# Keys and queries transposed on VectorE from a second load, and the last w2 slices loaded into w2's own room

## The chip, the cores and the metric

The kernel runs on one core of one Trainium2 chip. The metric is the device time of one execution in microseconds (us). Engines are named as in the profile: PE (TensorE, matmuls), PEld (its weight loads), DVE (VectorE), ACT (ScalarE), POOL (GpSimd) and SP (SyncE, which here only issues DMAs).

## The reference

A delta-rule recurrence over 4 batches, 8 heads, 768 steps and head width 48, whose output is laid out as x of 4 x 768 x 384, goes through a mixer: a low-rank mix over the sequence (U, V of rank 32) and a two-layer ReLU network of width 1536.

```python
def _attn_ref(q, k, v, beta):
    k_n = k / (np.linalg.norm(k, axis=-1, keepdims=True) + 1e-06)
    for t in range(S):
        y[:, :, t] = einsum('bhd,bhde->bhe', q[:, :, t], state)
        v_old = einsum('bhde,bhd->bhe', state, k_n[:, :, t])
        state = state + bt * einsum('bhd,bhe->bhde', k_n[:, :, t], v[:, :, t] - v_old)

def _moe_ref(x, U, V, w_ch1, w_ch2):
    h = x.transpose(0, 2, 1) @ U @ V
    u = x + h.transpose(0, 2, 1)
    return u + np.maximum(u @ w_ch1, 0.0) @ w_ch2
```

All matrices are float32 on the chip. The weights arrive as float64 and are put together from their two halves on the chip.

## The kernel before

**Units.** The recurrence is cut into chunks of L = 64 steps. A unit is half a batch, that is 6 chunks of 8 heads; units 0 to 7 are numbered n, and batch b has units 2b and 2b + 1. Keys of a unit come in by tokens (tile kn, 64 tokens by 48 numbers for each chunk and head, two heads stacked on the 128 partitions), queries likewise (qn), values too (vn).

**Within a unit.** `grams` makes the transposed keys and queries and their products. For each of three pairs of chunks, `key_pair` turns four 128x128 blocks of keys on PE against the identity (`turn`, L529, into PSUM tile p_t), ACT copies them to SBUF (L535, tile kq), and `products` multiplies keys by keys (L553, p_g), which ACT or DVE copies to pg. `query_pair` does the same with queries; DVE masks that product into qk (L569). `norms` squares the keys (L461), sums them on DVE (L464) and gets the scales, which go through DRAM (L499, L505, tiles scrc and cp) to where they are wanted. `blocks` takes pg through DRAM (L624, L635) into 96 rows of 32x32 blocks (gs), inverts these on DVE in 31 steps of two instructions (L668 prod, L674 xt; "inversion n" below), writes them to DRAM (L683), reads them back in two layouts (L707 zt, L710 zc), turns zc on DVE (L695 zn), and joins the 32-blocks into 64-blocks with two rounds of small matmuls (L722 p_x, L736 p_v), which ACT writes into zt (L746). For units 0 and 1 the inversion goes in 16-blocks, with `join` instead.

**Recurrence.** `recur(b)` walks through 12 chunks: keys and queries times state (L870, p_y), DVE takes it from the values (L900, rhs), p_s (L907), ACT copies z (L916), p_s and p_y (L921, L929), DVE adds the state (L944). It is a chain from chunk to chunk.

**Mixer.** `front(b, i)` mixes over the sequence: p_tt (L971), DVE copy tt (L977), p_tt again (L980), tt (L985), p_h (L995), DVE adds to x (L1001), PE turns x (L1005, p_u), ACT copies ut (L1008). `wide(b, i)` does the two layers on 384 tokens: 36 matmuls p_f (L1038) with ReLU on ACT, 36 p_o (L1058) with an addition on DVE (L1028) and a store by SP (L1029). The profile counts each of these float32 matmuls as two. These matmuls stand between the steps of the next batch's recurrence.

**Weights.** `load_weights` brings the weights in 14 slices (U, V, six of w1, six of w2; all but U have 768 columns) through POOL's queue, in turn into a tile of their own ("wide") and into the room of a later x ("stage", tag x). Each slice takes five DVE instructions and one on ACT. Until w2 is needed its room (`early`) holds other things: queries of unit 1, keys of unit 2, squares and small blocks. `recur(b)` for b > 0 waits for the last w2 slice, because its x takes stage's room.

**Order.** There is no scheduling at run time. A planner in the kernel (`run`) holds a clock for each engine. Every `step` states its cost, and among parts whose `need` is met the planner emits the one that can start first, with ties going to the lower place number given in `order`. So costs and places fix the order of each engine's queue once, when the kernel is built; at run time each engine takes its queue in order. SP's queue holds nearly all DMAs of keys, queries, values, of DRAM passes and of the output.

Of the kernel before, what the change touches and what calls it, by code (L numbers as in the profile page):

```python
# [27 lines left out]
def kernel(  # L28
# [157 lines left out]
    beta_sb = unit.tile([B * H, S], FP32, name="beta_sb", tag="kq")  # L186
# [94 lines left out]

    def load_weights():
# [6 lines left out]

        def start(i):  # L290
            dst, src, groups = slices[i]
            n = dst.shape[1]
            if i % 2:
                wide = stage[:, 0 : 2 * n].bitcast(I32).rearrange("p (n two) -> p n two", two=2)
            else:
                wide = conv.tile([128, n, 2], I32, name="wide")
            src = src.bitcast(I32)
            to = wide.rearrange("p n two -> p (n two)")
            if groups:
                to = to.rearrange("p (c r) -> p c r", c=groups)  # L300
                src = src.rearrange("(c p) r -> p c r", c=groups)
            copies = 128 // src.shape[0]
            yield step(pool=0.55 * copies)
            for c in range(copies):
                at = slice(c * 128 // copies, (c + 1) * 128 // copies)
                nc.gpsimd.dma_start(out=to[at], in_=src)
            loaded[i] = wide
            emitted(("landed", i), 6.0)

        def load_all():  # L310
            for i in range(len(slices)):
                yield need(("weights", i - 2), *[("v", 0)] * (i == 1), *[("opened", 1)] * (i == 2))
                yield from start(i)

        begin(load_all(), 2.03)
        for i in range(len(slices)):
            dst = slices[i][0]
            yield need(("landed", i))

            if dst.shape[1] == WIDE and i >= 2 + KT * DFF // WIDE:  # L320
                yield need(("ksq", 2), *[("keys turned", 2, c) for c in range(UC // 2)])
# [38 lines left out]
            emitted(("weights", i), 0.2)  # L360

# [54 lines left out]
    def load(n):  # L416

        yield need(("rec", n - 2))
        kq = unit.tile([128, UC, 2, 2, 2 * L], FP32, name="kq")
# [19 lines left out]
    def load_queries(n):  # L439
        yield need(("turned", n - 1), ("turned", 0))  # L440
        yield from fetch(n, "q", qn[:, :, :, 0:D], q, (0, 0))

    def norms(n):
# [8 lines left out]
        if n > 2:  # L452

            ksq = made[n][0][:, UC // 2 :].rearrange("p c j i t -> p (c j i t)")
        else:
            ksq = early[:, (1536, 2816, 0)[n] :]
# [59 lines left out]
    def grams(n, place):  # L516


        yield need(("k", n), ("room", n), ("pg", 0 if n == 1 else -1))
        kn = keys[n]  # L520
        kq, pg, qk = made[n]

        def turn(ts, places):
# [11 lines left out]
            nc.scalar.copy(places, p_t)  # L535

        def products(c0, i):
# [9 lines left out]
            for c in range(2):  # L547
                for j in range(2):
                    for par, x in QUADS:
# [5 lines left out]
                            kq[rows, c0 + c, j, 0, cols],  # L555
                            kq[rows, c0 + c, j, i, cols],
# [19 lines left out]
        def key_pair(c0):  # L576
            if n > 2 and c0 + 2 > UC // 2:
                yield need(("ksq", n))
            yield from turn([(kn, c0), (kn, c0 + 1)], kq[:, c0 : c0 + 2, :, 0])
            emitted(("keys turned", n, c0 // 2))  # L580
            yield from products(c0, 0)
            emitted(("p", n, c0 // 2), 0.5)

        def query_pair(c0):
            yield need(("q", n), ("p", n, c0 // 2))
            yield from turn([(qt, c0), (qt, c0 + 1)], kq[:, c0 : c0 + 2, :, 1])
# [13 lines left out]
        emitted(("turned", n))  # L600

# [264 lines left out]
    def recur(b):  # L866
        def from_state(p, kq, cu, i, s_old, first):

            for j, par, x in heads:
                nc.tensor.matmul(  # L870
                    p[half(x ^ par), par, D * (2 * i + j) : D * (2 * i + j) + D],
                    kq[half(par, D), cu, j, i, half(x)],
# [7 lines left out]
        yield need(("mixed", b - 2), ("rec", 2 * b - 1), w2_there(FT - 1 if b > 0 else -99))  # L880
# [198 lines left out]
    for n in range(2, 2 * B):  # L1079
        at = 0.01 * n + (3 if n < 4 else 5)  # L1080
        order += [(load_keys(n), at + 0.1), (load(n), at + 0.1), (load_queries(n), at + 0.5)]
# [39 lines left out]
```

## Time and profile before

| | |
|---|---|
| median of 8 runs | 680.02 us |
| lowest, highest | 676.44, 681.64 us |
| profiled execution | 676.58 us, of which 674.8 are the span that the profile shows |
| mean granted clock of PE | 0.919 of full speed |
| busy in the span | PE 92%, DVE 47%, ACT 29%, POOL 6% |
| chain of waits | PE 80%, DMA 7%, DVE 7% |
| DMA packets | 143893, of which 133952 on SP's queue |

The page has busy times by engine, forty equal slices of the span with a digit for the busy tenths, the chain of work that ended last, and groups of instructions by line. The trace answers more closely: instructions in order of time, with what ended an idle time in brackets, and busy times in chosen stretches. The profile is one execution, and a short one among the eight.

### The profile page before, as it was taken

How to read it: one execution, taken by the hardware profiler on the slowest of the kernel's cores; microseconds unless marked ns; L12 is line 12 of the kernel's file. 1: busy time of each engine (PE TensorE's matmuls, PEld its weight loads, DVE VectorE, ACT ScalarE, POOL GpSimd, SP SyncE). 2: the span in 40 equal slices, each digit the busy share in tenths (PEclk: the TensorE clock that was granted, in tenths of full speed). 3: DMA queues.
4: the chain of work that ended last, by engine and by line, in shares of the span. 5: the costliest groups of instructions: out<-in, count | busy, mean ns of one | idle time of the engine just before them, and what ended most of it. 6: DMA issues, size and time to landing. Idle time of an engine off the chain costs nothing.

```text
span 674.8 us, 19682 instructions
## 1 busy us (share of the span) xinstructions
PE 621.9 (92%) x8676; PEld 399.7 (59%) x8676; DVE 318.3 (47%) x795; ACT 199.0 (29%) x487; POOL 43.3 (6%) x84
## 2 busy tenths in 40 slices
PE   5639799859999999989999999999999999999997
PEld 4438688536555666556556655665655555555554
DVE  6667678579898124872942287368111011000000
ACT  2406456524221352144214322323221220110210
POOL 6442001100100000000000000000000000000000
PEclk9855555859999999999999999999999999999999
DMA  8586737742711332256033312420300000000000
GB/s 123 113 184 162 148 113 174 185 89 40 197 37 37 73 62 61 48 106 113 10 72 76 73 35 55 67 61 2 60 14 26 1 1 24 12 1 23 13 11 24
DMA packets 143893, 46.00 MB, mean 68 GB/s; under 512 B 136961, under 2 KB 140033, under 8 KB 143809
## 3 DMA queue, kind: packets, MB, share of 16 engines
q1 hardware_dynamic: 133952, 30.99, 22.6%
q0 software_dynamic: 3552, 12.88, 6.8%
q10 hardware_dynamic: 6304, 0.89, 0.8%
q8 instruction: 68, 1.11, 0.7%
q14 instruction: 17, 0.13, 0.1%
HBM read 33.62 MB, written 11.11 MB: 66 GB/s over the span
## 4 chain that ended last, share of the span: by engine, by line
PE 80%; DMA 7%; DVE 7%; ACT 2%; SPq 2%; issue 1%; ACTq 1%; DVEq 0%
PE p_o L1058 28%; PE p_f L1038 27%; PE p_y L870 4%; PE p_g L553 3%; PE p_t L529 3%; PE p_s L921 2%; PE p_s L907 2%; DMA scr<-xt 2%; PE p_y L929 2%; DVE xt L674 2%; DVE prod L668 2%; PE p_u L1005 1%; PE p_e L794 1%; DMA scr<-pg 1%; PE p_h L995 1%
## 5 line engine op out<-in xcount | busy, mean ns | idle before, releaser
L1038 PE MATMUL p_f<-ut,w_sb 128*128 128x384 f32 x576 | 202.3, 496 | 0.2 <-ACT h_f L1023 0.2
L1058 PE MATMUL p_o<-w_sb,h_f 128*128 128x384 f32 x576 | 201.1, 495 | 0.0
L1038 PEld LDWEIGHTS p_f<-ut,w_sb 128*128 128x128 f32 x576 | 104.3, 190 | 64.0 <-issue 0.6
L1058 PEld LDWEIGHTS p_o<-w_sb,h_f 128*128 128x128 f32 x576 | 104.6, 190 | 63.4
L1023 ACT ACTIVATE h_f<-p_f 128x384 f32<-128x384 f32 x96 | 47.1, 491 | 202.8 <-PE p_f L1038 202.7
L1028 DVE TENSOR_TENSOR x<-x,p_o 128x384 f32<-128x384 f32 x24 | 13.2, 553 | 131.4 <-PE p_o L1058 131.4
L674 DVE TENSOR_TENSOR xt<-xt,prod 96x112 f32<-96x112 f32 (+21 forms) x216 | 70.5, 326 | 7.4
L668 DVE TENSOR_TENSOR prod<-gs,xt 96x112 f32<-96x112 f32 (+21 forms) x216 | 70.0, 324 | 6.2
L553 PE MATMUL p_g<-kq 48*64 48x64 f32 x1536 | 40.2, 252 | 9.4 <-DVE qk L569 7.9
L944 DVE TENSOR_TENSOR s<-s,p_s 128x192 f32<-128x192 f32 x40 | 14.1, 352 | 69.2 <-PE p_s L921 68.9
L553 PEld LDWEIGHTS p_g<-kq 48*64 48x64 f32 x1536 | 33.8, 161 | 18.3 <-DVE qk L569 7.4
L951 ACT COPY x<-p_y 64x192 f32<-64x192 f32 x96 | 30.0, 313 | 39.2 <-PE p_y L929 34.0
L870 PEld LDWEIGHTS p_y<-s,kq 48*64 48x64 f32 x1408 | 28.8, 151 | 19.6 <-issue 10.9
L535 ACT COPY kq<-p_t 128x512 f32<-128x512 f32 x48 | 27.4, 587 | 38.6 <-PE p_t L529 38.4
L916 ACT COPY z<-p_s 128x192 f32<-128x192 f32 x48 | 15.3, 318 | 73.6 <-PE p_s L907 73.3
L900 DVE TENSOR_TENSOR rhs<-vn,p_y 128x192 f32<-128x192 f32 x44 | 15.5, 352 | 42.1 <-PE p_y L870 41.6
L870 PE MATMUL p_y<-s,kq 48*64 48x48 f32 x1408 | 34.3, 239 | 0.7 <-DVE s L944 0.5
L907 PEld LDWEIGHTS p_s<-rhs,zt 64*64 64x64 f32 x704 | 16.3, 148 | 21.8 <-issue 17.7
L921 PEld LDWEIGHTS p_s<-z,kn 64*64 64x64 f32 x704 | 16.0, 149 | 19.4 <-issue 16.5
L907 PE MATMUL p_s<-rhs,zt 64*64 64x48 f32 x704 | 21.9, 242 | 3.2 <-DVE qk L569 1.7
L794 PE MATMUL p_e<-zt,pg 64*64 64x32 f32 x192 | 12.0, 291 | 12.9 <-DMA zt<-scr 11.6
L637 POOL MEMSET xt<- 96x1056 f32 x6 | 5.9, 978 | 275.6 <-DMA scr<-xt 194.8
(122 smaller groups left out, 529.7 us busy)
## 6 DMA issues: line engine op xcount, KB each, us to landing
wide<-in_moe_w_ch_dram POOLq DMA_DIRECT2D x6, 768.0 KB, 5.3
stage<-in_moe_w_ch_dram POOLq DMA_DIRECT2D x6, 768.0 KB, 5.6
out_dram<-x SPq DMA_DIRECT2D x24, 192.0 KB, 2.2
kn<-in_k_dram SPq DMA_DIRECT2D x60, 72.0 KB, 2.4
qn<-in_q_dram SPq DMA_DIRECT2D x48, 72.0 KB, 3.1
vn<-in_v_dram SPq DMA_DIRECT2D x48, 72.0 KB, 2.7
gs<-scr SPq DMA_DIRECT2D x8, 384.0 KB, 4.7
scr<-xt SPq DMA_DIRECT2D x8, 384.0 KB, 4.5
```

The lines of the kernel that those rows point to most:

```text
L529: nc.tensor.transpose(p_t[:, x, j], t[:, c, 2 * j : 2 * j + 2].rearrange("p s d -> p (s d)"), ident,)
L535: nc.scalar.copy(places, p_t)
L553: nc.tensor.matmul(p_g[par][to, c, j], kq[rows, c0 + c, j, 0, cols], kq[rows, c0 + c, j, i, cols], start=True, stop=True,)
L668: nc.vector.tensor_tensor(out=prod, in0=gb[:, :, j : j + 1, j + 1 :].to_broadcast([NP, split, m, w]), in1=xb[:, :, 0:m, j : j + 1].to_broa ...
L674: nc.vector.tensor_tensor(out=xb[:, :, 0:m, j + 1 :], in0=xb[:, :, 0:m, j + 1 :], in1=prod, op=ALU.subtract,)
L870: nc.tensor.matmul(p[half(x ^ par), par, D * (2 * i + j) : D * (2 * i + j) + D], kq[half(par, D), cu, j, i, half(x)], s_old[half(par, D), ...
L907: nc.tensor.matmul(p_s[half(x), par, D * (2 + j) : D * (2 + j) + D], zt[half(x ^ par), cu, par, j], rhs[half(x ^ par), 2 * j + par], start ...
L921: nc.tensor.matmul(p_s[half(par), x, D * j : D * j + D], kn[half(x), cu, 2 * j + par], z[half(x), 2 * j + par], start=True, stop=True,)
L951: nc.scalar.copy(tokens_of(b, c, g), pair_of(p_y, 1)[half(g)])
L1023: nc.scalar.activation(hs[f], p_f, ACTF.Relu)
L1038: nc.tensor.matmul(p_f, w1_sb[:, t, f * 128 : (f + 1) * 128], ut[:, t], start=(t == 0), stop=(t == KT - 1),)
L1058: nc.tensor.matmul(p_os[c], hs[e][:, c * 128 : c * 128 + 128], w2_sb[:, e], start=(e == 0), stop=(e == FT - 1),)
```

## The change

For units 2 to 7, keys and queries are loaded once more, in pieces of 32 rows whose columns are blocks of 32 tokens, into the tile qn, which now serves as a staging place. One DVE instruction then turns all 32x32 blocks of the unit's keys at once into a tile kt, and one the queries into qt; PE's transposes and ACT's copies of these units are gone. Keys also still come in by tokens as before. Both loads share qn: a unit's queries come after its keys have been turned, the next unit's keys after its queries have been turned. The transposed tile kq becomes two tiles with the chunk as an inner dimension. Two of the six w2 slices are loaded into w2's own room once `early` is free, the last two both use "wide", and batch 1's recurrence no longer waits for w2. Conversion of weights is split into two parts with places of their own.

```diff
 def load_weights():
+        early_used = [("ksq", 2), ("below", 1, 2), ("turned", 1)]
         def start(i):
-            if i % 2:
+            if i in (W2 + 1, W2 + 3):
+                at = WIDE * (2 + (i - W2 + 1) // 2)
+                wide = early[:, at : at + 2 * n].bitcast(I32)
+                wide = wide.rearrange("p (n two) -> p n two", two=2)
+            elif i % 2 and i < W2:
                 wide = stage[:, 0 : 2 * n].bitcast(I32).rearrange("p (n two) -> p n two", two=2)
             else:
                 wide = conv.tile([128, n, 2], I32, name="wide")
 ...
         def load_all():
             for i in range(len(slices)):
-                yield need(("weights", i - 2), *[("v", 0)] * (i == 1), *[("opened", 1)] * (i == 2))
+                last = i - 2 if i < W2 + 5 else i - 1
+                yield need(("weights", last), *[("v", 0)] * (i == 1), *[("opened", 1)] * (i == 2))
+                if i == W2 + 1:
+                    yield need(*early_used)
                 yield from start(i)
 ...
+        begin(load_all(), 2.03)
+        begin(convert(range(W2 + 2)), 3.5)
+        begin(convert(range(W2 + 2, len(slices))), 4)
 ...
 def load(n):
-        kq = unit.tile([128, UC, 2, 2, 2 * L], FP32, name="kq")
+        kq = [unit.tile([128, 2, 2, UC, L], FP32, name=x) for x in ("kt", "qt")]
 ...
-    def load_queries(n):
-        yield need(("turned", n - 1), ("turned", 0))
-        yield from fetch(n, "q", qn[:, :, :, 0:D], q, (0, 0))
+    def turn_all(n):
+        b, hf = divmod(n, 2)
+        stage = qn.rearrange("p c s d -> p (c s d)")
+        places = stage.rearrange("p (x j m d) -> p x j m d", x=2, j=2, d=BK)
+        yield need(("queries turned", n - 1))
+        for i, (name, src) in enumerate((("keys", k), ("queries", q))):
+            for par in range(2):
+                for half_d in range(2):
+                    rows = slice(L * par + BK * half_d, L * par + BK * half_d + BK)
+                    ds = slice(BK * half_d, min(D, BK * half_d + BK))
+                    for x in range(2):
+                        yield step(sp=1.2)
+                        for j in range(2):
+                            h = 4 * (x ^ par) + 2 * j + par
+                            nc.sync.dma_start(
+                                out=places[rows, x, j, :, 0 : ds.stop - ds.start],
+                                in_=src[b, h, hf * UC * L : (hf + 1) * UC * L, ds].rearrange(
+                                    "(m t) d -> t m d", t=BK
+                                ),
+                            )
+            emitted((name, n), 8.0)
+            yield need((name, n), ("room", n), *[("ksq", n)] * (i == 1))
+            yield step(dve=1.8)
+            nc.vector.transpose(made[n][0][i].rearrange("p x j c t -> p (x j c t)"), stage)
+            emitted((name + " turned", n), 0.1)
 ...
 def grams(n, place):
         def products(c0, i):
-                            kq[rows, c0 + c, j, 0, cols],
-                            kq[rows, c0 + c, j, i, cols],
+                            kq[0][rows, x, j, c0 + c],
+                            kq[i][rows, x, j, c0 + c],
 ...
         def key_pair(c0):
-            if n > 2 and c0 + 2 > UC // 2:
-                yield need(("ksq", n))
-            yield from turn([(kn, c0), (kn, c0 + 1)], kq[:, c0 : c0 + 2, :, 0])
+            if n < 2:
+                yield from turn([(kn, c0), (kn, c0 + 1)], kq[0][:, :, :, c0 : c0 + 2])
 ...
         def query_pair(c0):
-            yield need(("q", n), ("p", n, c0 // 2))
-            yield from turn([(qt, c0), (qt, c0 + 1)], kq[:, c0 : c0 + 2, :, 1])
+            yield need(("q" if n < 2 else "queries turned", n), ("p", n, c0 // 2))
+            if n < 2:
+                yield from turn([(qt, c0), (qt, c0 + 1)], kq[1][:, :, :, c0 : c0 + 2])
 ...
 def recur(b):
-        yield need(("mixed", b - 2), ("rec", 2 * b - 1), w2_there(FT - 1 if b > 0 else -99))
+        yield need(("mixed", b - 2), ("rec", 2 * b - 1), ("weights", W2 - 1 if b > 0 else -1))
 ...
-        order += [(load_keys(n), at + 0.1), (load(n), at + 0.1), (load_queries(n), at + 0.5)]
+        order += [(load_keys(n), at + 0.1), (load(n), at + 0.1), (turn_all(n), at + 0.15)]
```

W2 is the number of the first w2 slice, 8 counted from 0. A built kernel has 16 key and 16 query DMAs per unit from `turn_all` (L475 in the changed kernel), of 32 partitions by 12 blocks by 32 numbers (16 for the upper half of the head width), where there were 8 query DMAs.

## The prediction

> **What bounds the kernel now.** First the page: busy shares and the forty slices, to find out who is full and when.
>
> ```profile
> span 674.8 us, 19682 instructions
> ...
> PE 621.9 (92%) x8676; PEld 399.7 (59%) x8676; DVE 318.3 (47%) x795; ACT 199.0 (29%) x487; POOL 43.3 (6%) x84
> ...
> PE   5639799859999999989999999999999999999997
> ...
> PEclk9855555859999999999999999999999999999999
> ```
>
> PE is full from slice 10 on, at full clock. Before that it is nearly full in places, but at half clock. So there are two stages; busy time by stretch shows the seam at 150 us, where the first p_f starts (150.57).
>
> ```profile
> 125.00:150.00 25.00, 15.37 (x232) 9.05 (x233) 15.48 (x40) 6.04 (x16) 0.70 (x1) 0.59 0.72 156
> 150.00:175.00 25.00, 23.82 (x248) 15.23 (x246) 22.79 (x59) 10.21 (x24) 0.00 (x0) 1.00 0.28 53
> ...
> 350.00:400.00 50.00, 50.00 (x897) 31.44 (x895) 19.00 (x50) 17.84 (x44) 0.00 (x0) 1.00 0.35 70
> ```
>
> The columns after the length are PE, PEld, DVE, ACT, POOL, then clock, DMA share, GB/s. From 150 to 650 all such stretches together leave PE idle for 6.9 us. In this **mixer stage** an instruction taken off PE is time taken off the end. In the **early stage** order of time shows who waits for whom just before the seam (timeline of DVE, then of PE):
>
> ```profile
> 135.68 1.22 DVE L652 TENSOR_TENSOR gs<-gs,cp 96x1024 f32<-96x1024 f32 x1 [6.50 <-DMA gs<-scr]
> ...
> 140.21 0.55 DVE L977 COPY tt<-p_tt 128x384 f32<-128x384 f32 x1
> ```
>
> ```profile
> 140.81 1.65 PE L980 MATMUL p_tt<-tt,quarters 128*128 128x384 f32 x2 [5.69 <-DVE tt L977]
> ```
>
> PE stands 5.7 us because the tt copy is queued on DVE behind gs of unit 2, whose DMA lands at 135.6. So the start of the mixer stage hangs on that landing.
>
> **What the Trainium skill says.** "VectorE: DVE Perf Modes", The three transpose paths: a TensorE transpose does 128x128 and ends in PSUM, a VectorE one does 32x32 blocks and ends in SBUF. The trace agrees: L529 is followed by a PSUM copy by ACT (L535, 587 ns for 512 columns), L695 by none. "DMA: Bandwidth & Descriptors", Why a DMA increments its semaphore by 16 and not by 1: the outermost sizes set how many of the 16 DMA engines a DMA uses, so 32 rows still use all 16. The 32x12x32 loads of L710, with the layout of the new loads, land in 2.1 us. "TensorE: Matmul & The Clock Gate", Part 1: the clock halves when PE has idled. Only partly so here: it is 0.50 from 40 to 110 us although PE is busy 9.5 of 10 us at 80 to 100, with small matmuls.
>
> **The change, part by part.** The built instruction order of both kernels was compared.
>
> *Removed from PE.* Transposes L529 of units 2 to 7: 6 units x 3 pairs x 2 x 4 = 144 of 192. A timeline in the mixer stage prices them:
>
> ```profile
> 381.59 1.09 PE L529 MATMUL p_t<-ident,qn 128*128 128x128 f32 x8
> 382.62 0.45 PE L921 MATMUL p_s<-z,kn 64*64 64x48 f32 x16
> ```
>
> Eight take 1.03 us to the next start, 0.13 each. Of the 144, 24 are unit 2 and 4 of unit 3 (at 144.7) in the early stage; 116 lie after the seam: **-15.1 us**, all on the path. The weight loads overlap and count nothing. The 36 ACT copies (36 x 0.587 = 21 us) go too; ACT is 29% busy and PE's own waits for them sum to 2.4 us over the whole run (p_ct 1.3, p_g 1.1): nothing.
>
> *Added to DVE.* Twelve transposes of 128x1536. Groups by shape:
>
> ```profile
> L695 DVE STREAM_TRANSPOSE zn<-zc 128x384 f32<-128x384 f32 x6 | 3.4, 574 | 6.4 <-DMA zc<-scr 6.3
> ...
> L695 DVE STREAM_TRANSPOSE zn<-zc 128x256 f32<-128x256 f32 x6 | 2.4, 425 | 3.1 <-DMA zc<-scr 3.1
> ```
>
> 128 more columns cost 149 ns, so 1536 cost 574 + 9 x 149 = 1.92 us, 23 us in all. DVE is at most 70% busy in the mixer stage but for 150 to 200 us (22.8 and 21.3 of 25). Nothing after 250 us; before that it is priced with the waits below.
>
> *Added to SP and the DMA engines.* Per unit 32 issues (keys 16, queries 16) in place of 8: 24 more at 0.50 us (L710, four in 2.01) to 0.98 us (vn at 103.17, eight in 7.86): 12 to 24, I take 0.62, 15 us. A unit comes every 60 us or so and SP issues about 25 us in it now, so there is room; order is the danger. Descriptors: 12288 for 3072. The queue's 22.6% of 16 engines over 133952 packets is 18.2 ns each, so 9216 more cost 10.5 us of all sixteen per unit, 0.18 of 60 us: the share 0.28 to 0.35 becomes about 0.5. Hidden.
>
> *Early stage, unit 2.* The 16 key issues stand on SP between zc and scr<-xt of unit 1 (43.4 and 58.95): 8 to 16 us into a gap of 15.5. They share the engines with zt<-scr, for which PE waits until 47.7: +1 us (0 to 3). The 16 query issues stand behind vn (ends 111.0) and ahead of scrc and scr<-pg of unit 2 (issued 113.0 and 122.8): they end at 119 to 126.7, I take 0.75 each, 123. So gs lands near 136 (135.6 to 139.5), and +0.3. Behind gs the new DVE order has the tt copy at once, where four inversion steps and qk stood (gs ends 136.9, tt starts 140.2): about -2.5, and without p_t and p_g between the p_u -1. In DVE's queue the first kt transpose stands before a recurrence rhs: +1 (0 to 1.9). The recurrence itself loses unit 2's transposes (4.5 us, 3 of them at half clock), but its end at 130 is not what the seam waits for. Without those wide matmuls the clock may stay at half from 118 on: up to +2. Sum **-2** (-4 to +5); the seam near 148.5.
>
> *w2's slices.* Two of the last six land in w2's own room, two conversions come before units' work (place 3.5 for 4), and recur(1) no longer waits for the last slice. That slice was done at 195.3, and the first p_s of recur(1) ran at 195.4: a wait is lifted, but unit 2's inversion holds the same instruction. The last two slices now share one buffer, so a 5.3 us load stands between their conversions; DVE has unit 3's inversion to do meanwhile. Nothing.
>
> *New waits in the mixer stage.* Inversion 2 runs 135.7 to 173.1 now. With kt of unit 3 in it (+1.9) and six qk moved out (6 x 0.37 = 2.2), and tt and x work ahead of it, it ends near 175. Its scr<-xt stands on SP behind unit 3's 16 query issues, which wait for that kt (about 164) and end at 174 to 175: just in time. Then DVE has two slices (8 us), qt 1.9 and zn, to about 186. PE gets to unit 3's query products at 148.5 + 36 p_f (23.2) + 12 p_o (7.7) + fronts and products (4.5) = 184, so it waits 1 us, then for p_v and the two ACT writes of zt (0.8 each) with nothing in between: 3 us. Inversion 3 starts behind slices and qk near 194 instead of 181 and ends near 229 (219.6 now), zt lands at 236, PE reaches its p_x near 234: 2.5 us. In-order PE can't pass either. Later units have p_f or p_o between the steps: 0 (to 3 each). Sum **+5.5** (0 to 20).
>
> *Sum:* -15.1 - 2 + 5.5 = -11.6 us. The profiled execution took 676.6 (span 674.8 and 1.8 around it), so 665.0; the median of eight lies 3.4 above it, which gives **668**.
>
> **Rivals.**
> 1. *Full gain.* The orders fit, the early stage gains its 4 us, no new wait: 676.6 - 15.1 - 4 + 3.4 = 661. For it: SP and DMA have room after 200. Against: DVE is 90% busy at 150 to 200.
> 2. *DVE becomes the bound around the seam.* Four transposes (7.7 us) lie in the work of units 2 and 3, all delay inversions, and PE waits them out besides the forecast's 5.5: 668 + 7.7 = 676. For it: 22.8 of 25. Against: qk moves out.
> 3. *Slower: the SP queue.* Every unit's scr<-pg, gs<-scr and scr<-xt, and through them its inversion, stand behind query issues that themselves wait for a DVE transpose. At 0.98 us an issue 16 take 15.7, not 10, so 5.7 late per unit; with five units after the seam up to 28 us, less what p_f and p_o cover. From 15.1 + 2 = 17 us, 3.4 a unit, it decides; at 5 a unit, 25 - 17 = +8: 688. A stand of 5 us also halved the clock at 130 to 150. For it: PE takes no instruction out of order. Against: 0.98 is seen only at DMA share 0.7, and SP waits on landings 8 issues back, which take 2 to 3 us after 200.
> 4. *Not what it says.* Excluded for PE: the built order has p_t for units 0 and 1 only.
>
> **How the numbers follow.** A measurement here tells 0.5% (3.4 us) from no change. Forecast 0.45, full gain 0.15, DVE 0.21 (half of it within 0.5%), SP queue 0.19. Faster 0.45 + 0.15 + 0.11 = 0.71, same 0.10, slower 0.19. The range of the forecast alone is 662 to 675. Leaving out the best 0.05 and the worst 0.15: 660 to 683.
>
> **What would show it.** Right: L573 p_t x48, p_t absent after the seam; DVE groups kt<-qn and qt<-qn of 1.9 us x6 each; seam at 146 to 151; idle of PE from the seam to 650 of 8 to 15 us, most before 240, put down to zt, qt or kt; packets near 199000. Wrong: the seam beyond 155 with gs landing past 142 (unit 2's SP order); stalls of PE for kt, qt or zt in units 4 to 7 (rival 3); DVE over 95% with p_g waiting for qt (rival 2).

## The result, and the profile after

The changed kernel takes **685.89 us** (median of 12 runs, 683.11 to 688.11), against 679.4 for the kernel before on the same chip: a ratio of **1.0097, 95% interval 1.0077 to 1.0118**. It is slower by some 6.5 us, where 668 was forecast, and outside the range (660 to 683). The ratios here and below count only runs within 1.5% of the fastest of their kernel; this matters most for e13 and e8, where two of six and seven of nineteen are left out, with which the ratios would be 0.993 and 0.995. The profiled execution, at 685.9, has 684.1 us of span against 674.8.

The changed kernel's page, its span, engines, and the slices of PE and of its clock:

```profile
span 684.1 us, 19552 instructions
...
PE 615.5 (90%) x8532; PEld 390.8 (57%) x8532; DVE 338.4 (49%) x807; ACT 179.4 (26%) x451; POOL 43.8 (6%) x84
...
PE   5448797789867989999899999999999999999997
...
PEclk9555555569968999999999999999999999999999
```

PE is busy 6.4 us less, and there are holes in slices 10 to 12 (171 to 222 us), with the clock down to six tenths. The same stretches as before, and two between (columns: length; PE, PEld, DVE, ACT, POOL busy; clock, DMA share, GB/s):

```profile
125.00:150.00 25.00, 18.52 (x232) 10.36 (x228) 16.93 (x35) 4.82 (x11) 0.70 (x1) 0.57 0.68 148
150.00:175.00 25.00, 24.50 (x173) 14.87 (x172) 20.55 (x52) 8.30 (x22) 0.00 (x0) 0.96 0.21 27
175.00:200.00 25.00, 17.15 (x368) 11.92 (x367) 19.59 (x34) 6.30 (x11) 2.68 (x3) 0.79 0.76 142
200.00:225.00 25.00, 20.96 (x244) 11.62 (x243) 19.15 (x50) 3.21 (x9) 0.42 (x1) 0.80 0.25 68
350.00:400.00 50.00, 49.70 (x845) 30.09 (x845) 24.68 (x65) 13.48 (x35) 0.97 (x1) 1.00 0.32 63
```

From 175 to 225 PE is idle for 11.9 us, and what it does runs at 0.8 of full clock. At 350 to 400 it is full again. So the loss has a place. Just before the seam, DVE and then PE in order of time:

```profile
136.38 1.22 DVE L700 TENSOR_TENSOR gs<-gs,cp 96x1024 f32<-96x1024 f32 x1 [4.06 <-DMA gs<-scr]
137.52 0.55 DVE L1025 COPY tt<-p_tt 128x384 f32<-128x384 f32 x1
```

```profile
138.12 1.53 PE L1028 MATMUL p_tt<-tt,quarters 128*128 128x384 f32 x2 [2.52 <-DVE tt L1025]
147.14 3.57 PE L1086 MATMUL p_f<-ut,w_sb 128*128 128x384 f32 x5
```

The tt copy follows gs at once, PE stands 2.5 us where it stood 5.7, and the seam is at 147.14 (150.57 before). But five p_f take 3.57 us: they start at half clock. The transposes, in the groups by shape:

```profile
L484 DVE STREAM_TRANSPOSE qt<-qn 128x1536 f32<-128x1536 f32 x6 | 10.7, 1775 | 5.9 <-DMA scrc<-cts 5.9
L484 DVE STREAM_TRANSPOSE kt<-qn 128x1536 f32<-128x1536 f32 x6 | 10.6, 1770 | 0.0
```

Now the hole: PE in order of time (lines left out run without a wait):

```profile
187.16 1.16 PE L600 MATMUL p_g<-qt,kt 48*64 48x64 f32 x64 [2.20 <-DVE qt L484]
...
193.20 1.13 PE L600 MATMUL p_g<-qt,kt 48*64 48x64 f32 x32 [3.93 <-DVE qk L616]
...
196.68 0.45 PE L955 MATMUL p_s<-vn,zt 64*64 64x48 f32 x4 [0.92 <-ACT zt L794]
...
211.80 2.93 PE L1106 MATMUL p_o<-w_sb,h_f 128*128 128x384 f32 x4 [3.17 <-DVE w_sb L367]
```

and what DVE and SP do meanwhile:

```profile
185.24 1.77 DVE L484 STREAM_TRANSPOSE qt<-qn 128x1536 f32<-128x1536 f32 x1
191.37 0.58 DVE L743 STREAM_TRANSPOSE zn<-zc 128x384 f32<-128x384 f32 x1 [4.36 <-DMA zc<-scr]
191.87 0.52 DVE L340 TENSOR_SCALAR power<-wide 128x768 uint16<-128x768 uint16 x1
192.31 1.41 DVE L616 TENSOR_TENSOR qk<-p_g,mask_u 128x256 f32<-128x256 f32 x4
```

```profile
168.47 9.03 SPq L475 DMA_DIRECT2D qn<-in_q_dram  x16
177.62 0.40 SPq L731 DMA_DIRECT2D scr<-xt  x1
178.11 2.86 SPq L672 DMA_DIRECT2D scr<-pg  x4
181.39 4.64 SPq L755 DMA_DIRECT2D zt<-scr  x4
186.07 2.06 SPq L758 DMA_DIRECT2D zc<-scr  x4
```

Read from the bottom: SP gives unit 3's 16 query loads, then scr<-xt of unit 2, then unit 3's scr<-pg, and only then zt and zc; zc lands at 191. In DVE's queue zn waits for it, and behind zn stand the last slice's power (L340) and qk. PE's third query product needs the PSUM room that qk frees. Behind it stands the whole recurrence of batch 1. That is the 3.93 us. scr<-pg (2.86 us) costs little of it, since zt can't start before scr<-xt has landed: it started 3.8 us after scr<-xt here and 3.1 before.

How much of the delay is SP's? The last step of inversion 2 and zn in the kernel before, and then that last step in the changed one:

```profile
172.87 0.21 DVE L674 TENSOR_TENSOR xt<-xt,prod 96x31 f32<-96x31 f32 x1
186.05 0.58 DVE L695 STREAM_TRANSPOSE zn<-zc 128x384 f32<-128x384 f32 x1 [2.74 <-DMA zc<-scr]
```

```profile
176.50 0.21 DVE L722 TENSOR_TENSOR xt<-xt,prod 96x31 f32<-96x31 f32 x1
```

zn is 5.3 us later. Of these gs brings 0.7 (136.38 for 135.68), inversion 2 takes 2.9 longer from there (1.8 of it is the transpose into kt), scr<-xt leaves SP 0.9 us after the inversion's end (177.62) instead of at once (173.14 before), and its way to zn takes 13.7 us instead of 12.9. So more than half is DVE's queue, and the 16 loads, which mostly ran while DVE was still at the inversion, cost 0.9.

The slice of w2 that is being converted at 191.87 (L340) is the last but one. Only when it is done is "wide" free: POOL loads the last slice at 197.18, DVE converts it from 207.87 to 211.75, and its p_o has waited 3.17 us.

**The account**, from the seam to the first p_f of the last batch (150.57 to 578.34 before, 147.14 to 587.60 after), in stretches of 5 us: PE's busy time times its clock 420.9 before and 407.0 after (**-13.9**), PE idle 6.8 and 21.2 (**+14.3**), and busy time lost to the lower clock 0.0 and 12.3 (**+12.3**). With -3.4 for the seam and +0.1 for the tail this is the 9.3 us between the spans.

"Lost" below is idle plus the share of busy time that the clock took away, from stretches of 2.5 us of the one profiled run:

| lost, us | 150 to 225 | 225 to 345 | 345 to 650 |
|---|---|---|---|
| before | 2.1 | 2.7 | 2.0 |
| changed | 20.1 | 9.8 | 2.1 |

After 345 us nothing more is lost than before, so no unit pays a price of its own there.

The 7.1 us more from 225 to 345 are mostly two stands in the middle of p_v and the halved clock behind them. The first, with one like it at 339.51 (1.85 us):

```profile
253.53 0.62 PE L784 MATMUL p_v<-xz,zn 32*32 32x32 f32 x49 [1.86 <-issue]
```

"issue" means that the profile shows nothing that PE waited for. Each stand follows some 230 small matmuls in a row, and behind each the clock is at half for 3.4 us. Each of the eight profiles below in which units 2 and 3 are turned on VectorE has one to three such stands of 0.9 to 2.3 us after the seam; the other twelve have none. So they belong to the price of the change, and what PE waits for in them stays open.

### The profile page after: what moved, and what is told of

Same layout as the page of the kernel before. It is cut to its first block, busy times and chain, and to the rows that moved or that the text cites. A ratio compares the mean times of both kernels' runs of the same rounds, so it can differ in the third digit from the quotient of the medians.

```text
span 684.1 us, 19552 instructions
## 1 busy us (share of the span) xinstructions
PE 615.5 (90%) x8532; PEld 390.8 (57%) x8532; DVE 338.4 (49%) x807; ACT 179.4 (26%) x451; POOL 43.8 (6%) x84
## 2 busy tenths in 40 slices
DMA packets 201494, 49.55 MB, mean 72 GB/s; under 512 B 194560, under 2 KB 197632, under 8 KB 201408
## 4 chain that ended last, share of the span: by engine, by line
PE 74%; DVE 9%; SPq 7%; DMA 6%; issue 2%; ACT 2%; ACTq 0%; DVEq 0%
PE p_o L1106 28%; PE p_f L1086 26%; PE p_y L918 4%; SPq L475 3%; PE p_g L600 3%; PE p_s L955 2%; PE p_s L969 2%; DVE prod L716 2%; DVE xt L722 2%; PE p_y L977 1%; PE p_u L1053 1%; DMA scr<-xt 1%; PE p_h L1043 1%; DMA kn<-in_k_dram 1%; SPq L408 1%
## 5 line engine op out<-in xcount | busy, mean ns | idle before, releaser
L1106 PE MATMUL p_o<-w_sb,h_f 128*128 128x384 f32 x576 | 207.7, 504 | 3.2 <-DVE w_sb L367 3.2
L1086 PEld LDWEIGHTS p_f<-ut,w_sb 128*128 128x128 f32 x576 | 107.4, 193 | 68.6 <-issue 3.6
L1076 DVE TENSOR_TENSOR x<-x,p_o 128x384 f32<-128x384 f32 x24 | 13.3, 554 | 115.0 <-PE p_o L1106 114.9
L600 PE MATMUL p_g<-qt,kt 48*64 48x64 f32 x768 | 20.1, 252 | 14.8 <-DVE qk L616 12.0
L918 PEld LDWEIGHTS p_y<-s,kt 48*64 48x64 f32 x704 | 17.7, 155 | 22.3 <-issue 16.1
L955 PEld LDWEIGHTS p_s<-rhs,zt 64*64 64x64 f32 x704 | 17.1, 153 | 21.4 <-issue 16.7
L969 PEld LDWEIGHTS p_s<-z,kn 64*64 64x64 f32 x704 | 16.7, 155 | 20.7 <-issue 16.4
L600 PEld LDWEIGHTS p_g<-qt,kt 48*64 48x64 f32 x768 | 17.3, 162 | 19.4 <-issue 10.7
L918 PE MATMUL p_y<-s,kt 48*64 48x48 f32 x704 | 23.5, 249 | 2.0 <-issue 1.6
L969 PE MATMUL p_s<-z,kn 64*64 64x48 f32 x704 | 22.4, 249 | 2.9 <-ACT z L964 2.9
L977 PE MATMUL p_y<-z,qk 64*64 64x48 f32 x768 | 23.0, 242 | 1.0 <-ACT z L964 1.0
L842 PE MATMUL p_e<-zt,pg 64*64 64x32 f32 x192 | 11.9, 291 | 12.8 <-DMA zt<-scr 11.7
```

Source lines behind the costliest of these rows:

```text
L600: nc.tensor.matmul(p_g[par][to, c, j], kq[0][rows, x, j, c0 + c], kq[i][rows, x, j, c0 + c], start=True, stop=True,)
L918: nc.tensor.matmul(p[half(x ^ par), par, D * (2 * i + j) : D * (2 * i + j) + D], kq[i][half(par, D), x, j, cu], s_old[half(par, D), x, j], ...
L955: nc.tensor.matmul(p_s[half(x), par, D * (2 + j) : D * (2 + j) + D], zt[half(x ^ par), cu, par, j], rhs[half(x ^ par), 2 * j + par], start ...
L969: nc.tensor.matmul(p_s[half(par), x, D * j : D * j + D], kn[half(x), cu, 2 * j + par], z[half(x), 2 * j + par], start=True, stop=True,)
L977: nc.tensor.matmul(p_y[half(x ^ par), par, D * (2 + j) : D * (2 + j) + D], qk[half(x), cu, par, j], z[half(x), 2 * j + par], start=(c == 0 ...
L1086: nc.tensor.matmul(p_f, w1_sb[:, t, f * 128 : (f + 1) * 128], ut[:, t], start=(t == 0), stop=(t == KT - 1),)
```

## The experiments

Differences between two kernels are differences of their ratios to the kernel before, times 679 us. T is the first unit that is turned on VectorE; the changed kernel has T = 2.

**Theories.** A: a chain of small stands at 182 to 222 us, each paid again by a clock that halves. A2, after the first four runs: PE's saved work is replaced by its own standing. N: the saving is real and new costs eat it. C: w2 alone. The forecast's rivals 2 (VectorE) and 3 (SP's queue) beside them.

### Which half of the change costs: e1, e2, e3, e13

e1 has w2's slices as before:

```diff
-            if i in (W2 + 1, W2 + 3):
 ...
-            elif i % 2 and i < W2:
+            if i % 2:
 ...
-                last = i - 2 if i < W2 + 5 else i - 1
-                yield need(("weights", last), ...
+                yield need(("weights", i - 2), ...
 def recur(b):
-        yield need(..., ("weights", W2 - 1 if b > 0 else -1))
+        yield need(..., ("weights", W2 + 5 if b > 0 else -1))
```

> The changed kernel with w2's slices as before: odd ones land in the room of x, recur(1) waits for the last slice, and conversion is one part again. Theory A (a chain of small stalls of PE from 182 to 222 us, each paid once more by a clock that falls to half): PE's wait of 3.2 us for the last w2 slice at 211.8 and the halved stretch behind it (2.4 us) go, recur(1) waits some 2 us longer in their place: 681 to 683 us, against 685.9 with the change whole. Theory B (w2's slices cost nothing, as forecast): 685 to 687. Theory C (the w2 edit is the whole cause): 666 to 670.

(In one thing the text is wrong: conversion stayed in two parts in the kernel that ran.)

e2 has w2's new slices and T = 8, that is, no unit on VectorE; e3 has w2 as in e1 and T = 4; e13 w2's new slices and T = 4. The main lines of it:

```diff
 def grams(n, place):
-            if n < 2:
+            if n < T:
                 yield from turn([(kn, c0), (kn, c0 + 1)], kq[0][:, :, :, c0 : c0 + 2])
 ...
-        order += [(load_keys(n), at + 0.1), (load(n), at + 0.1), (turn_all(n), at + 0.15)]
+        order += [..., (turn_all(n), at + 0.15) if n >= T else (load_queries(n), at + 0.5)]
```

> The other half alone: w2's slices in the new way, all keys and queries turned on PE as before and no second load. Theory A: the last slice is late here too, but unit 3's inversion and zn aren't behind a DVE transpose and 32 more issues, so PE has p_f and p_o left to cover most of it: 680 to 684 us, beside 679.4 before. Theory B (the slices cost nothing): 679 to 680. Theory C (they cost it all): 692 to 696, since PE's 14 us less are not there.

> w2's slices as before, units 2 and 3 turned on PE as before (one load of their queries), units 4 to 7 turned on VectorE from the second load. PE is rid of 96 transposes, 96 x 0.13 = 12.5 us, all in the mixer stage. Theory A (the loss lies at 147 to 222, in units 2 and 3): no stalls there, some 2 us at 300 to 316 stay: 667 to 671 us. The rival of SP's queue (every unit pays 5 us and more for its issues): four of six units pay, 679 to 688. The rival of VectorE as the bound speaks of units 2 and 3 only, and expects the same as theory A here.

> Units 4 to 7 on VectorE, units 2 and 3 on PE, and w2's slices in the new way. With w2 as before this stood at a ratio of 0.997 to the kernel before. If w2's slices cost what they cost alone (0.33%): 1.000, some 678 us. If they cost 0.98% whatever is around them, as in the changed kernel: 1.007, some 683 us.

| ratio to before (95%) | w2 as before | w2's new slices |
|---|---|---|
| no unit on VectorE | 1 | e2: 1.0033 (1.0011 to 1.0056) |
| units 4 to 7 | e3: 0.9970 (0.9946 to 0.9993) | e13: 0.9889 (0.9851 to 0.9928) |
| units 2 to 7 | e1: 0.9999 (0.9974 to 1.0024) | changed: 1.0097 (1.0077 to 1.0118) |

This table decides the study. Taking units 2 and 3 off VectorE makes the changed kernel some **14 us faster** (1.0097 to 0.9889), and 7.5 us faster than before, although PE then does 48 transposes more. With w2 as before the same step is worth 2 us. And w2's slices cost 2.2 us alone, 6.7 us in the changed kernel, and gain 5.5 where units 2 and 3 stay on PE. Theory A named the place rightly, but not the sizes: e1 (677.3 us) and e3 (676.2) lie outside every time that was named for them. The forecast's "Nothing" for w2 falls; so does C, and so does my expectation for e13, which knew only costs.

The stretch from 150 to 225 us, first of the changed kernel, then of e13:

```profile
150.00:225.00 75.00, 62.61 (x783) 38.41 (x781) 59.28 (x134) 17.82 (x41) 3.10 (x4) 0.85 0.41 79
```

```profile
150.00:225.00 75.00, 69.70 (x830) 41.17 (x829) 57.26 (x139) 19.00 (x41) 3.74 (x5) 0.98 0.39 83
```

PE 62.6 us busy at a clock of 0.85, against 69.7 at 0.98: lost 20.1 and 6.8 us. These 13.3 us are the larger part of the 20.0 between the two profiled executions, of which e13's is the fastest of its six. It isn't the wait for the last w2 slice, which e13 has as well. PE's timeline in e13, the start of batch 1's recurrence and that wait:

```profile
186.16 0.45 PE L963 MATMUL p_s<-vn,zt 64*64 64x48 f32 x16
...
195.93 2.42 PE L1114 MATMUL p_o<-w_sb,h_f 128*128 128x384 f32 x4 [2.99 <-DVE w_sb L369]
```

The recurrence starts at 186, ten us earlier than in the changed kernel, and zn runs 11.0 us earlier, at 180.35. gs of unit 2 brings 4.8 us of these (131.61 for 136.38), inversion 2 is 4.5 us shorter from there, without a transpose and with less ahead of it, scr<-xt leaves SP 0.8 us sooner behind it, and its way to zn is 0.9 shorter. Part of the 4.8 can be scatter: gs stands at 137.37 in e1 and at 132.17 in e15, which have the same order up to there. PE's other waits in the stretch sum to 2.3 us, 9.2 in the changed kernel. In e3, where recur(1) waits for w2's last slice as before, it starts at 199.06, and 36 p_o (as the profile counts) have run by then instead of 24. These p_o are what covers the recurrence. In e3 the last of them runs at 282.78 to 285.0, several steps before the recurrence ends; in e13 the stock lasts to 283.3, up to its last step. So w2's new rule (recur(1) doesn't wait) is worth something only if nothing else holds recur(1). This reading of the gain is from two timelines; no run isolates it.

### Is PE's saving real: e5, e9

Both put the saved transposes back as work that nobody reads, 4 ahead of every product: 96 in e3, 144 in the changed kernel.

```diff
 def products(c0, i):
+            if n >= T:
+                t = ps_one([128, 128], "idle")
+                for _ in range(4):
+                    nc.tensor.transpose(t, ident, ident)
```

> The kernel that turns units 4 to 7 on VectorE and has w2 as before (676.2 us), with 96 transposes of the identity that nobody reads put back on PE, four ahead of every product of a pair of those units: the 12.5 us of PE work that it had saved. All other queues keep their order. Theory A2 (PE's saved work was replaced by its own standing and by the halved clock that small matmuls keep, 290 to 307 us, so the end did not move): the added work fills the stand and holds the clock, 674 to 679 us. Theory N (PE's 12.5 us were saved, and the second load, SP or VectorE cost as much elsewhere): 686 to 690.

> The changed kernel itself (685.9 us) with all 144 saved transposes of units 2 to 7 put back on PE as transposes of the identity that nobody reads, four ahead of each product of a pair; they are worth some 19 us at full clock. Theory A2: 684 to 690 us, since they fill stands and hold the clock up. Theory N (new costs elsewhere, PE's saving is real): 698 to 705.

e5: 1.0185 (1.0144 to 1.0227), 14.6 us above e3, or 12.3 by the medians (688.5 and 676.2); 96 x 0.13 = 12.5. e9: 1.0318 (1.0258 to 1.0378), 15 us above the changed kernel. A2 falls, N holds: **PE's saving is real**, and what eats it is new cost.

### SP's queue: e8, e10, e11

```diff
 def turn_all(n):
-                            nc.sync.dma_start(
+                            nc.gpsimd.dma_start(
```

This goes into e3 (e8), the changed kernel (e10) and e1 (e11); PE, VectorE and ScalarE keep their order to the instruction.

> The same kernel (676.2 us) with the 32 loads per unit of the second copy issued on POOL's queue in place of SP's; PE, VectorE and ScalarE keep their order to the instruction, and SP gets rid of 128 issues. Rival 3 of the forecast (scr<-pg, gs<-scr and scr<-xt stand behind those issues on SP): 4 to 10 us faster, 666 to 672. Theory A2: SP is not what units 4 to 7 wait for, 674 to 678.

> The changed kernel (685.9 us) with the 32 loads per unit of the second copy issued on POOL's queue in place of SP's; PE, VectorE and ScalarE keep their order to the instruction, SP loses 192 issues. On POOL they stand between the loads of w1 and w2. Rival 3 of the forecast (SP's queue): the early chain and the stand at 185 to 197 us shorten, 676 to 681 us. Theory A2 (the loss is the late w2 slice, 6.7 us, and stands behind VectorE, each with a halved clock): 683 to 686 us; more than 687 if the loads of w2 come late behind those of the queries.

> The kernel with all transposes of units 2 to 7 on VectorE and w2 as before (ratio 1.000 to the kernel before, 678 us), with the second load on POOL's queue. In its profile PE waits 2.7 us for zt's load at 187 to 190 us, which stands on SP behind the query loads of unit 3, and the same queue cost 2.7 us in units 4 to 7. Rival 3: 670 to 674 us. If SP isn't what is waited for in units 2 and 3: 674 to 678.

e8: 0.9925 (0.9894 to 0.9956), 3 us better than e3, with intervals that overlap a little; that is less than the 4 to 10 us that rival 3 gave. e10: 1.0021 (0.9998 to 1.0044), **5.2 us better** than the changed kernel. e11: 1.0008 (0.9986 to 1.0029), no better than e1, against both expectations. What PE waited for most in e10, 150 to 225 us (engine and line, what it waited for, total us, times, longest):

```profile
PE p_o L1106 <- DVE w_sb L367: 3.2, 1, 3.2
...
PE p_g L600 <- DVE qk L616: 1.1, 1, 1.1
```

The wait for qk fell from 3.9 to 1.1 us (1.1 us of "issue" stand behind it); the others stayed. In this trace scr<-xt leaves SP 0.1 us after inversion 2, and zn follows 11.8 us later instead of 13.7: together the 2.8 us by which the wait for qk is shorter. The rest of the lead was there before; the seam is at 143.64. So SP's order was in the chain, and rival 3's mechanism exists. It isn't a price of every unit, since the changed kernel loses nothing from 345 to 650. The Trainium skill, "DMA: Bandwidth & Descriptors", Issuing engines are not separate DMA queues, says that another issuing engine saves only the issuing sequencer's time, usually little. Here it was 9.0 us for 16 loads on SP, and to move them was worth 5.2 us. SP's 5.2 us and w2's 6.7 don't add: with both taken away (e11) 6 us are gone. e11's trace shows what came in their place. scr<-xt leaves SP at once (172.44), but zc lands 16.6 us later, at 189.0, where it took 11.8 in e10; DVE stands 7.3 us there, and PE 8.2 in three waits. Two slices of w2 come in meanwhile, one in e10; that they slow the passage isn't shown.

### The clock: e4, e7, e14, e15, e12

e4 fills the stands at 185 to 193 in the changed kernel with 14 and 26 unread transposes:

```diff
 def products(c0, i):
+            if (n, i) == (3, 1) and c0 != 2:
+                idle = ps_one([128, 128], "idle")
+                for _ in range(14 if c0 == 0 else 26):
+                    nc.tensor.transpose(idle, ident, ident)
```

> The changed kernel with 40 transposes of the identity into an unused PSUM tile added on PE, 14 ahead of unit 3's first query products and 26 ahead of its third, where PE stands 2.2 and 3.9 us in the changed kernel. They are work that nobody needs: 40 x 0.13 = 5.2 us at full clock. Theory A (the clock falls because PE stands, and the halved clock of 187 to 202 costs 4 us on top of the stand): the clock is 0.9 or more in 187 to 202, and the time 682 to 684 us. Theory D (the clock falls for another reason, for instance what the matmuls are): the clock stays near half, the added work takes up to 10 us in a stand of 6, and the time is 686 to 690.

1.0114 (1.0074 to 1.0154): no gain. The clock did hold:

```profile
187.00:192.00 5.00, 4.59 (x181) 4.24 (x182) 1.60 (x4) 0.54 (x1) 0.00 (x0) 1.00 0.70 142
192.00:197.00 5.00, 2.53 (x135) 2.04 (x133) 4.78 (x10) 1.15 (x4) 0.71 (x1) 0.95 0.57 73
```

(0.75 and 0.50 in the changed kernel), but PE then stood later instead, 2.15 us in the middle of p_v with "issue" as its cause, and p_s began at 197.57 instead of 196.68. The gain that theory A expected from its second half, that each stand is paid twice, isn't there. As the new stand came in its place, the run doesn't settle what the halved clock costs here.

Another place is the front of batch 1. In e3, in two stretches:

```profile
285.00:290.00 5.00, 2.65 (x140) 2.30 (x144) 4.78 (x13) 0.94 (x3) 0.00 (x0) 1.00 0.22 61
290.00:308.00 18.00, 16.68 (x173) 8.83 (x166) 14.37 (x32) 5.81 (x15) 0.00 (x0) 0.53 0.53 90
```

PE stands 2.35 us in five, and then runs at half clock for 17 us while it is busy 16.7 of 18. e7 puts 24 unread transposes there (e14: 144 of 64x64 in their place; e15: as e7 in e1; e12: as e7 in e8):

```diff
 def products(c0, i):
+            # before: 4 at (n, i, c0) == (4, 1, 4) and at (n, i) == (5, 0); after: 8 at (4, 1, 2)
+            idle(before)
 ...
+            idle(after)
```

> The same kernel (676.2 us) with only 24 such unread transposes, 8 and 4 around the last two query products of unit 4 and 4 ahead of each key product of unit 5, where PE stood 3.7 us and the clock was half from 290 to 307 us. They cost 24 x 0.13 = 3.1 us at full clock. Theory A2 (in that stretch only matmuls of 128 by 128 bring the clock back, and the halved clock is on the path): the clock is 1.0 from 290 to 310 us and the time 668 to 672 us. If the halved clock there costs nothing, since VectorE and ScalarE hold the chain: 676 to 679 us.

> As the run with 24 unread 128 by 128 transposes in the front of batch 1, but with 144 unread transposes of 64 by 64 in their place: PE is kept busy about as long, with a quarter of the array. If the clock follows PE's standing: 1.0 from 290 to 307 us as with the large ones, 674 to 677 us. If small matmuls don't count, since the front's own are small too: half clock from 290 to 307 us as without, 676 to 682 us.

> All transposes of units 2 to 7 on VectorE and w2 as before (ratio 1.000), with the 24 unread transposes of 128 by 128 in the front of batch 1, where that kernel runs at half clock from 293 to 315 us and loses 9 us by it. If the clock is the cost there: it stays at 1.0 and the ratio falls to 0.990 to 0.996, 671 to 675 us. If the chain over VectorE and ScalarE is: 1.000 to 1.004.

> Units 4 to 7 on VectorE, w2 as before, second load on POOL's queue (673.5 us), and the 24 unread transposes in the front of batch 1 that took the halved clock away. A version meant to be fast. If both effects add: 671 to 674 us, as the 24 transposes paid for themselves and no more; a drop below 670 would say that the queue's waits and the clock's fall had hidden each other.

The stretch in e7, and, 7 us later in its run, in e14:

```profile
290.00:308.00 18.00, 14.71 (x230) 9.31 (x228) 16.70 (x38) 6.36 (x18) 0.00 (x0) 1.00 0.49 85
```

```profile
297.00:315.00 18.00, 16.51 (x282) 11.73 (x275) 13.04 (x28) 5.53 (x15) 0.00 (x0) 1.00 0.51 85
```

Both hold the clock at 1.0, so 64x64 holds it as 128x128 does; what the two share is that they fill stands. The other profiles agree. From 225 to 345 us the clock takes 7.9, 7.7, 10.6 and 11.0 us without filling (e3, e8, e1, e11), and 0, 0, 1.6 and 3.0 with it (e7, e14, e12, e15). e7 stands at 0.9963 (0.9939 to 0.9987), as e3: 24 transposes came for nothing, though e5's cost 0.13 us each. That misses my 668 to 672, since the gain is no larger than the price of the means. e15: 0.9951 (0.9916 to 0.9986), 3.3 us better than e1 in spite of 3 us of added work, with intervals that overlap. So the halved clock seems to cost some 3 us there, which pays for the filling and little more. e12: 0.9901 (0.9870 to 0.9933), 1.6 us below e8, which the intervals can't tell from nothing, and 7 below before, at the fast end of what I expected. e14: 1.0067 (1.0034 to 1.0100): 144 small ones take 9.0 us, and the time rises by 6.6 over e3, beyond both expectations.

### VectorE: e6, e18

Each transpose is done twice in a row; e6 in the changed kernel, e18 in e13 (units 4 to 7 only):

```diff
             nc.vector.transpose(made[n][0][i].rearrange("p x j c t -> p (x j c t)"), stage)
+            nc.vector.transpose(made[n][0][i].rearrange("p x j c t -> p (x j c t)"), stage)
```

> The changed kernel (685.9 us) with each of the twelve transposes on VectorE done twice in a row, 12 x 1.8 = 21 us more on that engine; the second one writes the same numbers again. Rival 2 of the forecast (VectorE is the bound around the seam): the four of units 2 and 3 add up to 7 us, more where the clock falls again: 691 to 696 us. If those stands hang on DMAs and on SP: 685 to 688. The eight of units 4 to 7 are expected to add nothing by either.

> Units 4 to 7 on VectorE, w2's slices in the new way (672.5 us), each of the eight transposes on VectorE done twice in a row, 8 x 1.8 = 14 us more on that engine, all of it after 225 us, where the forecast priced VectorE at nothing. If it is nothing: 671 to 674 us. If the fronts wait for VectorE as they did with all twelve done twice (half of what was added): 677 to 681 us.

e6: 1.0256 (1.0213 to 1.0298), 10.8 us for 21 us added. e18: 1.0036 (1.0014 to 1.0059), **10 us for 14 us added**, a rough number, since e13's interval is wide. PE's waits for kt after 225 us, in e13 and then in e18:

```profile
PE p_g L606 <- DVE kt L490: 1.0, 1, 1.0
```

```profile
PE p_g L607 <- DVE kt L491: 5.9, 4, 2.8
```

Done once, the eight make PE wait 1.0 us in all; done twice, 5.9, and after 225 us the clock takes 11.5 us instead of 3.3. My expectation for e6 that units 4 to 7 add nothing was wrong (from 345 to 650 us e6 loses 12.3 us, the changed kernel 2.1): the cover in the fronts is about one transpose deep.

### A version that beats both: e16, e17

e16 is e13 with the loads on POOL's queue; e17 adds 16 unread transposes in the front of batch 1.

> Units 4 to 7 on VectorE, w2's slices in the new way (ratio 0.989, 672.5 us), with the second load of units 4 to 7 on POOL's queue; w2's last two slices stand on POOL behind 16 key loads. If SP's queue costs here what it cost with w2 as before (3 us): a ratio of 0.984 to 0.987, 667 to 669 us. If that was the same loss as w2's: 0.988 to 0.991. A stand for w2's last slice longer than 3 us would turn it round: 0.993 and more.

> The same with 16 unread transposes of 128 by 128 in the front of batch 1, 4 ahead of the last query product of unit 4 and 4 ahead of each key product of unit 5, 16 x 0.13 = 2.1 us at full clock. Without them that front has 3.3 us of halved clock. So at most 1 to 2 us are to be had: within 0.3% of the run without them. If it is faster by more than that, the clock costs more than the profile of one run shows.

e16: **0.9829 (0.9785 to 0.9874), 666.1 us**, some 12 us faster than before and a little under the lowest time that I expected. In its profile 6.4, 3.2 and 2.3 us are lost in the three stretches of the table. e17: 0.9890 (0.9849 to 0.9931); 0.6% slower than e16, where I expected at most 0.3% either way, but the two intervals overlap. The transposes don't help.

With e16 there are four kernels with the second load on POOL's queue:

| ratio to before, loads on POOL | w2 as before | w2's new slices |
|---|---|---|
| units 4 to 7 | e8: 0.9925 | e16: 0.9829 |
| units 2 to 7 | e11: 1.0008 | e10: 1.0021 |

Beside the first table they say what SP's queue is worth. Taking units 2 and 3 off VectorE still gains 13 us with w2's new slices, where it gained 14. So most of the 14 us is not SP's queue. To move the loads gains 5.2 us with units 2 and 3 (e10) and 3.1 and 4.1 without (e8, e16). w2's slices cost 0.9 us in place of 6.7 where units 2 and 3 are on VectorE, and gain 6.5 where they aren't. Each of these differences is uncertain by some 3 us.

## Why the prediction was wrong, point by point

In the profiles the change came to +9.3 us where the sum said -11.6. Of the 21 us between, 12.3 are the clock in the mixer stage, a term that the sum doesn't have, 8.8 are new waits, 1.2 the work taken off PE, and the early stage is 1.4 on the good side.

- **Removed from PE, -15.1: right.** -13.9 in the account; 48 p_t are left (L573), all before the seam; e5 and e9 confirm the price.
- **Early stage, -2: right in its steps, one profile thin in its size.** gs was awaited until 136.4, the tt copy followed at once, and the seam moved by -3.4. But e15, whose early code is that of e1, has its seam at 141.4 against 147.5, so a single profile doesn't fix this term. All profiles together do: the seam lies at 141.4 to 147.7 in the eight with units 2 and 3 on VectorE (mean 145.8) and at 146.6 to 155.7 in the twelve with them on PE (151.8). The early stage gains some 6 us. The clause "up to +2" for a clock that stays at half came true: the first 5 us of p_f ran at 0.52.
- **Added to DVE: size right, cover unnamed.** 1.77 us, not 1.92. "Nothing after 250 us" held for the wait for kt (1.1 us, at 306.24), but e18 shows that it held by a margin of about one transpose. DVE's busy share, from which I took it, says nothing about the fronts, where DVE, ACT and PE take turns.
- **Added to SP and DMA: "hidden" was wrong for SP's order.** Issues took 8.9 to 13.5 us for 16, where 10 to 12 were priced, and 201494 packets came. "Just in time" for unit 2's scr<-xt was nearly right (177.62 after 176.7). What the loads cost in all, 5.2 us (e10), is more than this 0.9; where the rest of it lies isn't shown. zn at 191 instead of 186.05, which holds qk, is for the larger part DVE's, as read above.
- **w2's slices, "Nothing": wrong.** "DVE has unit 3's inversion to do meanwhile" named the cover and not the one who waits. The shared buffer put the last slice's load behind a conversion that itself stood behind zn, so the slice was done at 211.75 instead of 195.36. No rule waited for it any more, but its p_o did. 2.2 us alone, 6.7 with units 2 and 3 on VectorE, 0.9 with the loads off SP (e10 against e11).
- **New waits, +5.5 (0 to 20): the step that failed.** I had 3 us at recur(1) and 2.5 at unit 3's p_x. Idle time rose by 14.3: 7.9 at recur(1) and 3.2 for w2 in its wake; most of the rest are the two stands without a known cause, 3.7. The range of this term held it, the value taken did not. The failing step is "qt 1.9 and zn, to about 186": it has zn run when DVE is free, and DVE was, at 187.0. It leaves out the passage of zt and zc through DRAM behind scr<-xt. With scr<-xt at 175 and the 12.9 us that this takes in the kernel before, zn would have been due at 188; it took 13.7 from 177.62, and zn ran at 191.37. And it leaves out the queue behind zn: qk, with PE's third query product behind it.
- **The clock: a term left out, with no reason given.** 12.3 us of the account. I named the halved clock for stands of 5 us, in a rival only; stands of 1.9 to 4 us did it. That rival misread the kernel before: its clock is at half from 129.3 us on, ahead of the stand of 5.7 us at 135 to 141, after 3.3 us in which PE was busy for 1.58. How much of the 12.3 us is on the path isn't settled: e4 found no gain, e7 and e15 point to some 3 us in another front.
- **Rivals.** Rival 3 came nearest in time (688), by luck: the loads cost 5.2 us in all, not 5 per unit, and the loss lies before 345 us. Rival 2's premise, four transposes in a full stretch, was part of it: inversion 2 is 2.9 us longer.

**What stays open.** SP's queue is a small part of the 14 us. How the rest divides between DVE's queue, DMA traffic, the stands without a known cause and the halved clock behind them can't be said: no run takes one of these away alone. Why zc's passage is slow in e11 isn't shown. The place of the seam scatters by several us between kernels with the same early order, and no run says why.

The Trainium skill, "TensorE: Matmul & The Clock Gate", Part 1, has the clock fall after a whole idle window of about 3.4 us and return after a busy one. The length agrees: the halved stretches are multiples of 3.41 us, 3.41 behind each stand of 1.9 us in the changed kernel and 17.07 in e3. The rule doesn't: those 1.9 us were enough, as were 2.35 us spread over 5 us in e3, and 16.7 busy of 18 us didn't bring the clock back in e3. The measurement decides.

## What to carry to other kernels

Work taken off the full engine is a gain only where the engines that feed it don't fall behind for it. Look for the stretch where all of them are busy at once, and leave the change out there (here units 2 and 3, worth 13 to 14 us). When a wait is priced, follow the data's whole way and the queue behind the waiting instruction, and allow for a clock that may halve behind it. Loads that wait for room are better on a queue where nothing urgent stands behind them (3 to 5 us in three of four pairs here).

## What the runs showed of the hardware

- After 2.35 us of standing in 5 us PE's clock stayed at half for 17 us with PE over 90% busy (e3, 290 to 307 us); 24 transposes of 128x128 or 144 of 64x64, put into the stands, kept it at 1.0 (e7, e14). The Trainium skill, "TensorE: Matmul & The Clock Gate", Part 4: PE-mode transpose, says that PE's transpose mode doesn't count as busy for the clock in the same way. These transposes did hold the clock; whether they run in that mode the trace doesn't show, it records them as MATMUL.
- A stand of 1.86 us at 253.5 us, in the middle of otherwise busy work, was followed by 3.41 us at half clock (changed kernel).
- 144 transposes of 64x64 kept PE busy for 9.0 us (62 ns each, e14), 24 of 128x128 for 3.6 us (150 ns, e7): a quarter of the array at two fifths of the price.
- A transpose of 128x1536 on VectorE took 1.77 us, one of 128x384 0.57 us: four times the columns, three times the price.
- The loads on POOL's queue cost 617 ns of POOL each, 78 us in all for the 128 of e16, and the time still fell (666.1 us, e13 672.5).
